# Making GpSimd wait for the VectorE copy planned before it, in an attention and gated-MLP kernel

## The chip, the cores and the metric

One core of a Trainium2 chip. The metric is the device time of one execution, in microseconds (us). A kernel was timed in several executions, and its median is quoted. On one core an execution can only be told to be slow against others of the same kernel. TensorE, VectorE (DVE in the profile), ScalarE (ACT), GpSimd (POOL) and the DMA queues are busy at the same time in the traces. The program joins them by semaphores; this case is about one more place where two of them meet.

## The reference, cut to what matters

The input has 2048 rows of 512 values. Attention with 32 heads of 16 values runs beside a gated bilinear layer of 1376 columns, and a sigmoid gate mixes the two.

```python
def reference(A_x, A_wqkv, A_wo, B_x, B_w_gate, B_w_up, B_w_down, gate_w):
    ...
        scores = jnp.einsum("bhqd,bhkd->bhqk", q, k) * (Dh ** -0.5)
        p = _softmax(scores, axis=-1)            # 32 heads x 2048 x 2048
        o = jnp.einsum("bhqk,bhkd->bhqd", p, v)
    ...
        h = g * u                                # g, u: x times w_gate, w_up
        return jnp.einsum("bsf,fd->bsd", h, w_down)
    ...
    g = _sigmoid((x * gate_w).sum(-1, keepdims=True))
    return g * a + (1 - g) * b
```

The costly part is the exponential of 134 million scores (32 x 2048 x 2048).

## The kernel before

About three quarters of the exponentials are real ones on ScalarE (line 1446). The others are made on VectorE by integer arithmetic: a score plus a constant, written as int16, has the bits of a bfloat16 power. One such operation reads PSUM (line 919, 512 columns). Three further variants of the result, with other fractional offsets, are needed; they are SBUF-to-SBUF additions on int16 (`32.0 * k`, k = 1 to 3) that the kernel calls copies. VectorE makes most of them (line 975, two tiles of 512 columns at once); GpSimd makes nearly all of those with k = 3 (line 978; 243 of 246 pairs of tiles). GpSimd also scales V (line 607) and normalises the attention output (line 1107).

No order is written by hand. The kernel file contains a planner: a small simulation with a clock for each engine, run on the host while the program is built. Whatever it decides becomes the order of each engine's queue. Which instruction waits for which comes from a list of dependencies alone. Planned times do not bind anything: on the chip, an instruction starts when its engine is free and its dependencies are met.

The planner's own rule keeps the VectorE copies and all GpSimd work apart in time, through `lock`:

```python
        def gen_step(eng):                        # one step of dve, pool, sp
            t = clock[eng]
            best = None
            if eng == "pool" and t < lock["dve"]: # a VectorE copy is running: wait
                clock[eng] = lock["dve"]
                return True
            ...                                   # best = a ready task of this queue
            if eng in ("dve", "pool") and (best is None or best.prio > 2.5):
                if eng == "pool" or lock["pool"] <= t:   # GpSimd is running: no copy
                    c = try_copy(eng, t)          # k = 1..3 on VectorE, k = 3 on GpSimd
                    if c is not None:
                        run_task(c, t)
                        lock[eng] = clock[eng]
                        return True
            ...
            qs[eng].remove(best)
            run_task(best, t)
            if eng == "pool":
                lock["pool"] = clock["pool"]
            return True
```

and in `try_copy`, the two forms of a copy (`n` is 2 but for the last one):

```python
            if eng == "dve":
                fn = lambda v: v.tensor_single_scalar(cell_ap(c, n, I16), cell_ap(pr["cell"], n, I16), 32.0 * k, ALU.add)
            else:
                fn = lambda g: g.tensor_scalar(cell_ap(c, n, I16), cell_ap(pr["cell"], n, I16), 32.0 * k, 1.0, ALU.add, ALU.mult)
            return _Task(eng, pr["p1"] + old, fn, occ, cb=cb)   # waits for its inputs and for free cells
```

The softmax here doesn't subtract the row's maximum and nothing guards it: scores larger than these inputs give would overflow.

Of the kernel before, what the change touches and what calls it, by code (L numbers as in the profile page):

```python
# [180 lines left out]
def bass_gated_mix__mha_block__glu_gated_bilinear__prompt_kernel(  # L181
    nc: bass.Bass,
    A_x: bass.AP,
    A_wqkv: bass.AP,
    A_wo: bass.AP,
    B_x: bass.AP,
    B_w_gate: bass.AP,
    B_w_up: bass.AP,
    B_w_down: bass.AP,
    gate_w: bass.AP,  # L190
    out: bass.AP,
):
    _build(nc, A_x, A_wqkv, A_wo, B_w_gate, B_w_up, B_w_down, gate_w, out)


def _build(nc, A_x, A_wqkv, A_wo, W_gate, W_up, W_down, gate_w, out):
# [29 lines left out]
    with ExitStack() as stack:  # L226
# [46 lines left out]
        def ready(task):  # L273
            r = 0.0
            for d in task.deps:
                if d.end is None:
                    return None
                e = d.end + (0.0 if d.eng == task.eng and not d.dma else SEM)
                if e > r:
                    r = e  # L280
            return r

        def run_task(task, t):
            ops = [d.op for d in task.deps]
            task.op = P.op(task.eng, task.fn, ops, task.stream, 16 if task.dma else 1)
            task.start = t
            task.end = t + task.lat
            clock[task.eng] = t + task.occ
            LOG.append(task)
            if task.cb:  # L290
                task.cb(task)
            return task
# [147 lines left out]
        PLAT = 0.44  # L440
        SW = 0.11
        pe = {"mode": "c"}
        lock = {"dve": 0.0, "pool": 0.0}

        def pe_run(deps, fn, occ, mode, t, lat=None, cb=None):
            sw = SW if mode != pe["mode"] else 0.0
# [1010 lines left out]
        def gen_step(eng):  # L1457
            t = clock[eng]
            best = None
            if eng == "pool" and t < lock["dve"]:  # L1460
                clock[eng] = lock["dve"]
                return True
            for k in qs[eng]:
                if best is not None and k.prio >= best.prio:
                    continue
                r = ready(k)
                if r is not None and r <= t:
                    if k.alloc is not None:
                        old = k.alloc(t)
                        if old is None:  # L1470
                            WHY.append((t, "p1cell"))
                            continue
                        k.deps = k.deps + old
                        k.alloc = None
                    best = k
            if eng in ("dve", "pool") and (best is None or best.prio > 2.5):
                if eng == "pool" or lock["pool"] <= t:
                    c = try_copy(eng, t)
                    if c is not None:
                        run_task(c, t)  # L1480
                        lock[eng] = clock[eng]
                        return True
            if best is None:
                return False
            qs[eng].remove(best)
            run_task(best, t)
            if eng == "pool":
                lock["pool"] = clock["pool"]
            return True
# [28 lines left out]
        for f, bk in ((f_k(0, 0, 0), slots[0][2]), (f_q(0, 0, 0), slots[1][2])):  # L1518
# [4 lines left out]
            while st["fill"] is not None:  # L1523
                do_fill(clock["pe"])

        steps = {"pe": pe_step, "act": act_step, "dve": lambda: gen_step("dve"), "pool": lambda: gen_step("pool"), "sp": lambda: gen_step("sp")}
        engs = ["pe", "act", "dve", "pool", "sp"]
        while True:
# [7 lines left out]
        def drain():  # L1536
            for _ in range(100000):
                live = [e_ for e_ in ("act", "dve", "pool", "sp") if qs[e_]]
                if not live:
                    return  # L1540
                e_ = min(live, key=lambda x: clock[x])
                if not gen_step(e_):
                    clock[e_] += 0.02
# [4 lines left out]
        c = NCH - 1  # L1548
# [19 lines left out]
        for tt in range(4):  # L1568
            cs = slice(tt * 128, (tt + 1) * 128)
            a1 = now("act", [lastpv, free], lambda a, cs=cs: a.activation(lnd[:, cs], DB.ap[:, cs], ACT.Ln), 0.2)  # L1570
            a2 = now("act", [a1], lambda a, cs=cs: a.activation(rlast[:, cs], lnd[:, cs], ACT.Exp, scale=-1.0), 0.2)  # L1571
            mt = now(
                "dve",
                [a2] + oxfree.get((NB - 1) % 2, []),
                lambda v, cs=cs: v.tensor_tensor(OX[:, (NB - 1) % 2, cs], psO[:, cs], rlast[:, cs], ALU.mult),
                0.2,
            )
            o = pe_run(
                [mt],
                col(banks[tt].ap, OX[:, (NB - 1) % 2, cs], woz[:, 1, :], False, True),  # L1580
                PACK,
                "c",
                clock["pe"],
            )
            combine(4 * c + tt, banks[tt].ap, o)
            while qs["dve"] or qs["sp"]:
                for e_ in ("dve", "sp"):
                    if qs[e_] and not gen_step(e_):
                        clock[e_] += 0.02
# [31 lines left out]
```

## Time and profile before

| | before |
|---|---|
| median of 3 runs | 803.12 us |
| profiled run, first to last instruction | 797.8 us |
| ScalarE / VectorE / TensorE / GpSimd busy | 734 / 711 / 712 / 332 us |
| mean granted TensorE clock | 0.973 |

From the page of the kernel before: the busy time of each engine; the busy tenths of VectorE and ScalarE in 40 equal slices of the execution; and three groups of instructions (line, engine, operation, output<-input, shapes, count, then busy us and mean ns, then idle time before them and what ended it).

```profile
PE 711.6 (89%) x9149; PEld 206.4 (26%) x9149; DVE 711.2 (89%) x1255; ACT 734.4 (92%) x710; POOL 331.5 (42%) x334
...
DVE  3889997789999999999999999998798999888983
ACT  3999898799999899999999999999999999889987
...
L1446 ACT ACTIVATE PT<-psS 128x1024 bf16<-128x1024 f32 (+1 forms) x572 | 614.5, 1190 | 44.5 <-PE psS L861 28.9
L978 POOL TENSOR_SCALAR PT<-PT 128x1024 int16<-128x1024 int16 x243 | 273.0, 1125 | 355.5 <-DVE PT L919 190.5
...
L975 DVE TENSOR_SCALAR PT<-PT 128x1024 int16<-128x1024 int16 (+1 forms) x498 | 276.1, 594 | 7.9 <-PE psO L1035 2.3
```

ScalarE is the busiest engine, VectorE and TensorE follow closely, and GpSimd is idle for 356 us before its copies. The 594 ns of line 975 is a mean over very unequal instructions; the view of this one line gives a minimum, median and maximum of 285, 418 and 1475 ns. Taken alone, the form with 1024 columns (groups of lines kept apart by shape, same columns):

```profile
L975 DVE TENSOR_SCALAR PT<-PT 128x1024 int16<-128x1024 int16 x495 | 275.4, 596 | 7.9 <-PE psO L1035 2.3 <-PE psS L1046 1.1
```

Why do some copies take three times as long as others of the same shape? Here is one pair, from the timelines of VectorE and of GpSimd in the same 3.5 us (start, length, engine, line; `x2` merges two in a row; the bracket has the idle time before and what ended it):

```profile
270.00 0.68 DVE L919 TENSOR_SCALAR PT<-psX 128x512 int16<-128x512 f32 x1
270.72 1.61 DVE L975 TENSOR_SCALAR PT<-PT 128x1024 int16<-128x1024 int16 x2
272.25 0.68 DVE L919 TENSOR_SCALAR PT<-psX 128x512 int16<-128x512 f32 x1
```

```profile
270.84 1.21 POOL L978 TENSOR_SCALAR PT<-PT 128x1024 int16<-128x1024 int16 x1 [1.70 <-DVE PT L919]
```

Two VectorE copies, which need 0.75 us when undisturbed (the median of 86 such pairs), take 1.61. A GpSimd copy came in 0.12 us after the first had started; the second copy is drawn out until 0.28 us after the GpSimd copy ends. A blocked VectorE instruction does not show as idle time. It shows as a longer busy one, which is why the busy share hides it.

Last, the windows view of the kernel before: busy us of each engine in each stretch of 100 us.

```profile
core 0: us, PE busy (x) PEld busy (x) DVE busy (x) ACT busy (x) POOL busy (x), PEclk, DMA share, GB/s
200.00:300.00 100.00, 90.43 (x1173) 25.15 (x1173) 97.84 (x166) 95.39 (x90) 43.89 (x38) 1.00 0.06 18
300.00:400.00 100.00, 86.23 (x1096) 24.38 (x1096) 96.92 (x169) 93.64 (x87) 44.56 (x39) 1.00 0.06 18
400.00:500.00 100.00, 95.73 (x1232) 26.09 (x1228) 93.21 (x170) 99.01 (x99) 44.20 (x39) 1.00 0.06 20
500.00:600.00 100.00, 94.56 (x1157) 25.14 (x1157) 91.43 (x167) 98.53 (x100) 43.01 (x38) 1.00 0.05 14
```

VectorE is the fullest engine from 200 to 400 us, ScalarE from 400 to 600. A kernel can have a different limit in each stretch.

Two measures, worked out from the traces instruction by instruction, are used below. *Blocked time* is, summed over the line 975 copies longer than 430 ns, what they take above 418 ns. *Lost exponential time* is, summed over the exponentials of line 1446, how much later each started after the previous one than the back-to-back pace (0.903 us at 1024 columns, 1.330 at 1536). Before, blocked time is 89 us and lost exponential time 67 us.

### The profile page before, as it was taken

How to read it: one execution, taken by the hardware profiler on the slowest of the kernel's cores; microseconds unless marked ns; L12 is line 12 of the kernel's file. 1: busy time of each engine (PE TensorE's matmuls, PEld its weight loads, DVE VectorE, ACT ScalarE, POOL GpSimd, SP SyncE). 2: the span in 40 equal slices, each digit the busy share in tenths (PEclk: the TensorE clock that was granted, in tenths of full speed). 3: DMA queues.
4: the chain of work that ended last, by engine and by line, in shares of the span. 5: the costliest groups of instructions: out<-in, count | busy, mean ns of one | idle time of the engine just before them, and what ended most of it. 6: DMA issues, size and time to landing. Idle time of an engine off the chain costs nothing. (4 is left out here: it accounts for less than half of the span.)

```text
span 797.8 us, 21597 instructions
## 1 busy us (share of the span) xinstructions
PE 711.6 (89%) x9149; PEld 206.4 (26%) x9149; DVE 711.2 (89%) x1255; ACT 734.4 (92%) x710; POOL 331.5 (42%) x334
## 2 busy tenths in 40 slices
PE   7998879988888899888799999999999988889894
PEld 3323322322222222222222222222222222222221
DVE  3889997789999999999999999998798999888983
ACT  3999898799999899999999999999999999889987
POOL 2543643144443444444435434444343444344430
PEclk9999997999999999999999999999999999899887
DMA  9700000000000010000000100000001000000000
GB/s 178 254 16 3 18 16 19 2 14 20 16 17 17 3 39 21 19 16 18 15 5 18 35 26 16 18 16 16 6 15 32 29 19 16 11 10 15 18 16 27
DMA packets 31015, 21.66 MB, mean 27 GB/s; under 512 B 18344, under 2 KB 25928, under 8 KB 30920
## 3 DMA queue, kind: packets, MB, share of 16 engines
q1 hardware_dynamic: 26936, 18.44, 7.9%
q10 hardware_dynamic: 3984, 1.84, 1.1%
q8 instruction: 73, 1.20, 0.6%
q14 instruction: 22, 0.18, 0.1%
HBM read 15.11 MB, written 2.35 MB: 22 GB/s over the span
## 5 line engine op out<-in xcount | busy, mean ns | idle before, releaser
L1446 ACT ACTIVATE PT<-psS 128x1024 bf16<-128x1024 f32 (+1 forms) x572 | 614.5, 1190 | 44.5 <-PE psS L861 28.9
L978 POOL TENSOR_SCALAR PT<-PT 128x1024 int16<-128x1024 int16 x243 | 273.0, 1125 | 355.5 <-DVE PT L919 190.5
L861 PE MATMUL psS<-QM,KE 32*128 32x512 bf16 x1732 | 273.4, 391 | 17.1 <-ACT PT L1446 9.5
L975 DVE TENSOR_SCALAR PT<-PT 128x1024 int16<-128x1024 int16 (+1 forms) x498 | 276.1, 594 | 7.9 <-PE psO L1035 2.3
L1035 PE MATMUL psO<-PT,VS 128*18 128x512 bf16 x1791 | 241.0, 390 | 6.1 <-DVE PT L975 2.7
L919 DVE TENSOR_SCALAR PT<-psX 128x512 int16<-128x512 f32 x316 | 214.6, 679 | 28.1 <-PE psS L861 24.8
L1035 PE MATMUL psO<-PT,VD 128*18 128x512 bf16 x1479 | 227.6, 387 | 9.2 <-DVE PT L975 4.8
L861 PE MATMUL psX<-QM,KE 32*128 32x512 bf16 x316 | 122.5, 388 | 24.6 <-DVE PT L919 10.9
L1446 ACT ACTIVATE wv<-psS 128x1024 bf16<-128x1024 f32 (+1 forms) x117 | 134.1, 1160 | 6.7 <-PE psS L861 6.2
L919 DVE TENSOR_SCALAR PT<-psS 128x512 int16<-128x512 f32 x177 | 118.8, 679 | 11.2 <-PE psS L861 9.0
L861 PEld LDWEIGHTS psS<-QM,KE 32*128 32x128 bf16 x1732 | 67.4, 91 | 167.6 <-ACT PT L1446 68.4
L1035 PE MATMUL psO<-wv,VS 128*18 128x512 bf16 x257 | 71.9, 393 | 1.3 <-POOL PT L978 1.0
L1035 PEld LDWEIGHTS psO<-PT,VS 128*18 128x18 bf16 x1791 | 56.7, 89 | 62.8 <-issue 31.8
L861 PEld LDWEIGHTS psX<-QM,KE 32*128 32x128 bf16 x316 | 28.7, 91 | 152.2 <-DVE PT L919 71.9
L1035 PEld LDWEIGHTS psO<-PT,VD 128*18 128x18 bf16 x1479 | 52.6, 88 | 56.9 <-issue 32.7
L492 PE MATMUL psS<-xT,wu 128*32 128x512 bf16 x672 | 55.1, 391 | 2.2 <-DVE hT L707 1.3
L492 PE MATMUL psS<-xT,wg 128*32 128x512 bf16 x672 | 52.6, 384 | 3.8 <-DVE PT L919 1.4
L492 PE MATMUL psS<-wd,hT 128*32 128x512 bf16 (+1 forms) x704 | 53.0, 386 | 2.3 <-DVE PT L919 2.3
L1107 POOL TENSOR_TENSOR OT<-oraw,rb 128x512 bf16<-128x512 f32 x16 | 20.6, 1284 | 38.2 <-DMA rb<-rscr 38.1
L675 DVE CAST usb<-psS 128x512 bf16<-128x512 f32 (+1 forms) x43 | 29.1, 677 | 1.8 <-PE psS L492 1.8
L707 DVE TENSOR_TENSOR hT<-psS,usb 128x512 bf16<-128x512 f32 (+1 forms) x43 | 29.1, 677 | 1.7 <-PE psS L492 1.6
L1107 POOL TENSOR_TENSOR OX<-oraw,rb 128x512 bf16<-128x512 f32 x15 | 19.1, 1272 | 23.1 <-DMA rb<-rscr 23.1
(87 smaller groups left out, 339.1 us busy)
## 6 DMA issues: line engine op xcount, KB each, us to landing
rb<-rscr SPq DMA_DIRECT2D x31, 256.0 KB
out_dram<-ost SPq DMA_DIRECT2D x16, 128.0 KB, 1.7
wu<-in_B_w_up_dram SPq DMA_DIRECT2D x1, 1376.0 KB, 7.5
wg<-in_B_w_gate_dram SPq DMA_DIRECT2D x1, 1376.0 KB, 10.6
wd<-in_B_w_down_dram SPq DMA_DIRECT2D x1, 1280.0 KB, 12.4
OT<-OX SPq DMA_DIRECT2D x60, 16.0 KB, 1.8
wv<-in_A_wqkv_dram ACTq DMA_DIRECT2D x2, 256.0 KB, 7.8
wo<-in_A_wo_dram SPq DMA_DIRECT2D x1, 512.0 KB, 8.6
```

The costliest lines, as they stand in the source:

```text
L492: return e.matmul(out_ap[32 * q : 32 * q + w, :], lhs[:, 32 * q : 32 * q + w], rhs, start=s0, stop=s1, tile_position=(0, 32 * q), skip_gro ...
L675: lambda v: v.tensor_copy(usb[0:w, n % 2, :], bk.ap[0:w, :]),
L707: lambda v: v.tensor_tensor(hT[0:w, f, :], bk.ap[0:w, :], usb[0:w, n % 2, :], ALU.mult),
L861: r = e.matmul(bk.ap, KE[32 * j : 32 * j + 32, b, kt * 128 : (kt + 1) * 128], QM[32 * j : 32 * j + 32, p, b, :], start=True, stop=True, ti ...
L919: lambda v: v.tensor_scalar(cell_ap(pr["cell"] + i, 1, mybir.dt.int16), bk.ap, CB, 0.0, ALU.add, ALU.max),
L975: fn = lambda v: v.tensor_single_scalar(cell_ap(c, n, I16), cell_ap(pr["cell"], n, I16), 32.0 * k, ALU.add)
L978: fn = lambda g: g.tensor_scalar(cell_ap(c, n, I16), cell_ap(pr["cell"], n, I16), 32.0 * k, 1.0, ALU.add, ALU.mult)
L1035: r = e.matmul(psO[32 * j : 32 * j + VW, :], pv_stationary(m, kt, j, k), cell_ap(cell, 1), start=s0, stop=s1, tile_position=(0, 32 * j), s ...
L1107: lambda e: e.tensor_tensor(dst, oraw[:, s, :], rb[:, s, :], ALU.mult),
L1446: lambda a: a.activation(cell_ap(c, n), src, ACT.Exp, scale=LN2 / 128.0),
```

## The change

The intent: the planner keeps GpSimd and the VectorE copies apart, but the chip does not know it. So each GpSimd operation is given one dependency more, on the VectorE copy planned last before it.

```diff
-        lock = {"dve": 0.0, "pool": 0.0}
+        lock = {"dve": 0.0, "pool": 0.0, "op": None}
...
                     c = try_copy(eng, t)
                     if c is not None:
+                        if eng == "dve":
+                            lock["op"] = c
+                        elif lock["op"] is not None:
+                            c.deps.append(lock["op"])
                         run_task(c, t)
...
             qs[eng].remove(best)
+            if eng == "pool" and lock["op"] is not None:
+                best.deps.append(lock["op"])
             run_task(best, t)
```

The planner's decisions do not depend on it. The work and the order of every queue stay as they were. Only GpSimd's waits change.

## The prediction

> **What bounds the kernel now.** The page gives ScalarE 734 us busy (92% of 797.8), VectorE 711 (89%), TensorE 712 (89%), GpSimd 332 (42%). In the trace, back-to-back exponentials (line 1446) start 0.903 us apart at 1024 columns and 1.330 us at 1536; the 689 of them would take 698 us at that pace, but stretch over 764: 67 us are lost. The windows view shows where. From 200 to 400 us VectorE is the limit: 98 and 97 us busy per 100, ScalarE 95 and 94, 17 us of exponential time lost. From 400 to 600 ScalarE is 99% busy and loses 7 us.
>
> **Why VectorE is so full.** Its 495 SBUF-to-SBUF copies of 1024 columns (line 975) last 418 ns in the median but 596 in the mean. Setting them against the GpSimd spans: 168 copies start while a GpSimd operation is already running; they average 948 ns and end some 0.28 us after it. 113 overlap but started first; they average 419 ns. The Trainium skill (SBUF — State Buffer, section "SBUF: two separate sides") says that GpSimd and a VectorE operation in a two-port mode take an exclusive lock and the loser fully blocks. This trace agrees: the copies pay 89 us above 418 ns. Matched to the planned order, 158 of 241 GpSimd copies start before the copy planned ahead of them has ended, typically by 1.5 us: the plan keeps the two apart but doesn't enforce it. Pairs in the wrong order cost 67 us of the 89; the other 22 are copies that overtake a GpSimd operation planned before them.
>
> **What the change does.** No instruction and no order changes; GpSimd's waits rise to a later VectorE count. GpSimd operations of the wrong order start 1 to 1.5 us later; with 356 us idle before its copies it can afford that. It removes about 67 us of blocked copies and gives some back: GpSimd now starts right behind a copy and holds the lock about 1.05 us; two PSUM reads of VectorE (0.598 us apart) cover that, one doesn't. From the order and these durations I estimate 10 us of that, on top of the 22. So VectorE falls from 711 to about 655 us busy, and 25 to 45 us of blocking remain.
>
> **How much is on the critical path.** Only where VectorE limits. If 200 to 400 us loses as little as 400 to 600, that is 10 us; 600 to 750, where 20 us are blocked and 15 of exponential time lost, perhaps 8; 100 to 200, where TensorE's projections and a lower clock matter too, perhaps 4; the rest 1. Sum about 23 us.
>
> **Predicted: 780 us, range 768 to 793.** Chances: faster by over 2% 0.78, within 2% 0.20, slower by over 2% 0.02.
>
> **What would show it.** Right: line 975 copies near 480 ns in the mean; blocked excess under 45 us; VectorE about 655 us busy, ScalarE 94 to 95%; GpSimd copies waiting for line 975; TensorE's waits for GpSimd results under 20 us. Wrong: the copies' mean stays above 550 (collisions only moved to the next copy); or the mean falls but 200 to 400 us loses the same exponential time (something else limits); or TensorE waits for GpSimd tiles.
>
> **What would make it wrong.** Delayed GpSimd operations may hit the next copy instead; later tiles may hold TensorE or tile cells longer; a denser TensorE may be granted a lower clock (0.973 now, 0.90 to 0.93 in two stretches).

## The result, and the profile after

| | before | after |
|---|---|---|
| median of 4 runs | 802.41 us | 771.93 us |
| profiled run | 797.8 us | 767.6 us |
| mean granted TensorE clock | 0.973 | 0.977 |
| blocked time of the line 975 copies | 89 us | 30 us |
| lost exponential time | 67 us | 37 us |

The ratio of after to before is 0.962, with a 95% interval of 0.959 to 0.965: faster. Ratios here and below divide the mean time of one kernel's fast runs by that of the other's in the same rounds, so they are not quite the ratio of the medians. Executions over 1.5% slower than the fastest of the same kernel are left out of the means.

The same lines of the page after:

```profile
PE 707.3 (92%) x9149; PEld 207.6 (27%) x9149; DVE 658.8 (86%) x1255; ACT 727.6 (95%) x710; POOL 314.4 (41%) x334
...
DVE  3889896689898999999989989898788989989882
ACT  3999988898999999999999999999999999999987
...
L1446 ACT ACTIVATE PT<-psS 128x1024 bf16<-128x1024 f32 (+1 forms) x572 | 614.2, 1240 | 25.9 <-PE psS L861 13.0
L978 POOL TENSOR_SCALAR PT<-PT 128x1024 int16<-128x1024 int16 x243 | 256.1, 1055 | 359.7 <-DVE PT L975 226.4
...
L975 DVE TENSOR_SCALAR PT<-PT 128x1024 int16<-128x1024 int16 (+1 forms) x498 | 217.2, 476 | 6.6 <-PE psO L1035 1.2
```

The instruction counts are the same. VectorE does the same work in 52 us less busy time: line 975 fell by 59, and a few us came back in other lines. GpSimd's idle time before its copies hardly grew (355.5 to 359.7 us), but what ends it has changed: the VectorE copy, line 975. GpSimd's copies became shorter too (1125 to 1055 ns), since a GpSimd copy that arrives during a VectorE copy is blocked in its turn: before, the 136 that started during one averaged 1190 ns, the other 107 averaged 1043; after, only 8 started during one. ScalarE waits 26 us in place of 45 at line 1446.

The same pair of copies after, with the GpSimd copy of the same place in the plan:

```profile
263.29 1.14 DVE L975 TENSOR_SCALAR PT<-PT 128x1024 int16<-128x1024 int16 x2
264.74 0.69 DVE L919 TENSOR_SCALAR PT<-psX 128x512 int16<-128x512 f32 x1 [0.30 <-PE psS L861]
```

```profile
262.78 1.04 POOL L978 TENSOR_SCALAR PT<-PT 128x1024 int16<-128x1024 int16 x1 [1.76 <-DVE PT L975]
264.52 1.04 POOL L978 TENSOR_SCALAR PT<-PT 128x1024 int16<-128x1024 int16 x1 [0.69 <-DVE PT L975]
```

The GpSimd copy starts at 264.52, behind both VectorE copies, which end at 264.43, and beside operations that read PSUM. What blocking remains is also to be seen: the first of the two VectorE copies met the GpSimd copy before this one, which ran until 263.82, and the pair took 1.14 us in place of 0.75.

And the windows:

```profile
200.00:300.00 100.00, 95.19 (x1248) 26.73 (x1240) 91.66 (x175) 99.03 (x96) 43.66 (x40) 1.00 0.07 22
300.00:400.00 100.00, 92.95 (x1198) 26.55 (x1190) 93.21 (x183) 99.79 (x94) 44.45 (x42) 1.00 0.05 15
400.00:500.00 100.00, 97.43 (x1224) 26.13 (x1221) 91.89 (x176) 99.93 (x103) 41.94 (x39) 1.00 0.07 23
500.00:600.00 100.00, 95.62 (x1187) 25.78 (x1184) 85.71 (x163) 99.05 (x100) 40.83 (x38) 1.00 0.06 17
```

From 200 to 400 us ScalarE is now 99% busy, as it already was from 400 to 600. VectorE has handed the limit to ScalarE there.

Set against the planned times (the planner was run on the host, and its list paired with the trace in the order of each queue), the execution before fell further and further behind: 2.5 us behind at the start, 21 us at 400 us, 37 us near the end of the main part. After, it stays 4 to 6 us behind from 200 to 720 us. That is a picture of what happened, not yet a proof of its cause.

### The profile page after: what moved, and what is told of

Same layout as the page of the kernel before. It is cut to its first block, busy times and chain, and to the rows that moved or that the text cites. A ratio compares the mean times of both kernels' runs of the same rounds, so it can differ in the third digit from the quotient of the medians.

```text
span 767.6 us, 21608 instructions
## 1 busy us (share of the span) xinstructions
PE 707.3 (92%) x9149; PEld 207.6 (27%) x9149; DVE 658.8 (86%) x1255; ACT 727.6 (95%) x710; POOL 314.4 (41%) x334
## 5 line engine op out<-in xcount | busy, mean ns | idle before, releaser
L978 POOL TENSOR_SCALAR PT<-PT 128x1024 int16<-128x1024 int16 x243 | 256.1, 1055 | 359.7 <-DVE PT L975 226.4
L975 DVE TENSOR_SCALAR PT<-PT 128x1024 int16<-128x1024 int16 (+1 forms) x498 | 217.2, 476 | 6.6 <-PE psO L1035 1.2
L1446 ACT ACTIVATE wv<-psS 128x1024 bf16<-128x1024 f32 (+1 forms) x117 | 138.2, 1201 | 2.1 <-PE psS L861 2.0
```

Source lines behind the costliest of these rows:

```text
L1446: lambda a: a.activation(cell_ap(c, n), src, ACT.Exp, scale=LN2 / 128.0),
```

## The experiments

Two theories were put against each other. The *lock theory*: GpSimd and a VectorE copy exclude each other; GpSimd in the wrong order blocks copies; and a blocked copy costs time only where VectorE limits. Its rivals: that holding GpSimd back helps in some other way (pacing), that enforcing the plan from either side would do, and that every microsecond of blocking costs the same. All runs had 5 rounds. In each set of four they shared one chip and the runs of the kernel before. The medians of before in the three sets were 803, 800 and 803 us.

| run | ratio to before (95% interval) | blocked time |
|---|---|---|
| the change (first measurement) | 0.962 (0.959 to 0.965) | 30 us |
| e1_copies_only | 0.968 (0.963 to 0.973) | 32 us |
| e2_others_only | 1.002 (0.997 to 1.008) | 89 us |
| e3_dve_waits | 1.045 (1.040 to 1.050) | 79 us |
| e4_both_wait | 0.994 (0.989 to 0.999) | 0 us |
| e5_short_before (wrong result) | 0.956 (0.952 to 0.960) | 17 us |
| e6_short_after (wrong result) | 0.956 (0.953 to 0.960) | 11 us |
| e7_middle | 0.984 (0.980 to 0.988) | 70 us |
| e8_later | 0.997 (0.992 to 1.002) | 73 us |
| f0_after_again | 0.965 (0.962 to 0.969) | 28 us |
| f1_tail | 0.959 (0.956 to 0.963) | 31 us |
| f2_tail_fill | 0.947 (0.943 to 0.951) | 28 us |
| f3_wait_copies | 0.979 (0.975 to 0.983) | 5 us |

### Which GpSimd operations carry the gain: e1 and e2

The edits to the changed kernel, each taking away one of the two new waits (first e1, then e2):

```diff
-            if eng == "pool" and lock["op"] is not None:
-                best.deps.append(lock["op"])
```

```diff
-                        elif lock["op"] is not None:
-                            c.deps.append(lock["op"])
```

> Only the GpSimd copies (line 978) wait for the latest VectorE copy; the normalising multiplies and the V scalings do not. Lock theory (GpSimd in the wrong order blocks VectorE copies): before, 93 of the 99 wrong-order blockings and 66 of their 67 us came from GpSimd copies, so nearly the whole gain stays: ratio to before 0.960 to 0.967, blocked excess 28 to 34 us. Rival (any holding back of GpSimd, or the changed waits of the multiplies, is what helps): clearly less gain, 0.97 or more.

> Only the other GpSimd operations (multiplies, V scalings) wait for the latest VectorE copy; the GpSimd copies do not. Lock theory: under 1 us of wrong-order blocking came from them, so almost nothing: ratio 0.996 to 1.003, blocked excess 85 to 90 us, mean of the line 975 copies 585 to 600 ns. Rival: if the multiplies' timing carried the gain, 0.98 or less.

The wait of the GpSimd copies alone gives a ratio of 0.968, just outside the expected 0.960 to 0.967, with an interval that overlaps that of the full change (0.965 when it was run again). With the three slow runs of the kernel before left in, it would be 0.966, so this miss says little. The wait of the others alone gives nothing: 1.002, and the copies' mean stays at 595 ns. The gain is that of the GpSimd copies.

### Whether it is the length of the hold: e5 and e6

In the kernel before and in the changed one, GpSimd's copies were cut to 128 of 1024 columns. Their outputs are wrong, which doesn't matter for the times. The plan and the waits stay, and the target cells are cleared once at the start so that nothing unwritten is read.

```diff
-  g.tensor_scalar(cell_ap(c, n, I16), cell_ap(pr["cell"], n, I16), 32.0 * k, 1.0, ALU.add, ALU.mult)
+  g.tensor_scalar(cell_ap(c, n, I16)[:, 0:128], cell_ap(pr["cell"], n, I16)[:, 0:128], 32.0 * k, 1.0, ALU.add, ALU.mult)
```

> Wrong result on purpose: the kernel before, with the GpSimd copies doing 128 columns of 1024 (about 0.3 us in place of 1.04; the same plan, the same waits, the target cells cleared once at the start). No new wait. Lock theory (the time that GpSimd holds the lock is what costs): blocked excess falls from 89 to under 25 us and the time to 0.955 to 0.972 of before. Rival (the wait paces GpSimd or TensorE's order in some other way): no wait is added, so 0.99 to 1.0.

> Wrong result on purpose: the changed kernel with the same short GpSimd copies as e5. Lock theory: with short holds the wait has nothing left to save: within 0.6% of e5_short_before, 0.955 to 0.970 of before. Rival (the wait helps by pacing): 2 to 4% faster than e5_short_before.

Both came out at 0.956, medians 765.2 and 765.4 us. With short holds and no new wait, the kernel before is as fast as the changed one; with short holds the wait adds nothing. Pacing as the cause is ruled out: e5 has none, and e6 has it and gains nothing from it. How long GpSimd holds a copy up is what cost the time. One thing more differs in e5: short copies also hand their results on sooner. That can't be the main part: TensorE's waits for GpSimd results were about 15 us in all before the change and about 15 after it, and the change gained 30 us without shortening them. The changed kernel lies at 0.962 to 0.965 on two chips, within about 1% of this pair; that hints at how little the remaining blocking costs, but it is no bound, since e6 still has 11 us of blocking and the pair ran on another chip.

### Where a blocked microsecond costs time: e7 and e8

The change for the GpSimd operations planned from 190 to 380 us (e7) or from 380 to 600 us (e8) alone; both new waits got the condition, shown for e7:

```diff
-                        elif lock["op"] is not None:
+                        elif lock["op"] is not None and 190.0 <= t < 380.0:
```

> The change only for GpSimd operations planned between 190 and 380 us (about 200 to 400 us of the execution before). Critical-path theory (blocking costs time only where VectorE limits): this stretch lost 23 us of blocking to the change and gives 11 to 15 us, ratio 0.981 to 0.987. Rival (every us of blocking costs alike, 30 us of time for 60 of blocking): also about 11 us; the pair with e8_later tells them apart by time gained per us of blocking removed.

> The change only for GpSimd operations planned between 380 and 600 us (about 400 to 625 us before), where ScalarE was 99% busy. Critical-path theory: about 11 us of blocking go, but only 1 to 4 us of time: ratio 0.995 to 0.999, under 0.35 us of time per us of blocking. Rival (every us of blocking costs alike, 0.5): 5 to 6 us, ratio 0.992 to 0.994.

In e7, 19 us of blocking went and the ratio is 0.984: 1.6% of 800 us, 13 us. In e8, 17 us of blocking went (the expectation had said 11) and the ratio is 0.997: about 2 us, and its interval contains 1. By these totals that is 0.68 us of time for each blocked us where VectorE was the limit and 0.13 where ScalarE was. But the totals also hold what differed by chance outside the stretch. Counted by planned time inside it, e7 took away 21.0 us of blocking and 11.6 us of lost exponential time, 0.55 us per us; e8 took away 12.7 and 3.4, 0.27 per us. The full change gives 0.56 and 0.31 in the same two stretches. So a blocked us cost about twice as much where VectorE was the limit, and it was not free where ScalarE was. The rival of equal worth had expected 0.992 to 0.994 for e8; the interval just touches it at 0.992. With the 12.7 us that went in the stretch, equal worth at 0.5 would have been 6 us, again 0.992: e8's time alone makes equal worth unlikely but does not exclude it, and the counts by stretch speak against it.

### Enforcing the order from the other side: e3, e4 and f3

In e3, VectorE copies wait for the latest GpSimd operation planned before them, and GpSimd waits for nothing new. In e4, both sides wait. In e4 the edit to the changed kernel is:

```diff
                         if eng == "dve":
                             lock["op"] = c
-                        elif lock["op"] is not None:
-                            c.deps.append(lock["op"])
+                            if lock["gop"] is not None:
+                                c.deps.append(lock["gop"])
+                        else:
+                            lock["gop"] = c
+                            if lock["op"] is not None:
+                                c.deps.append(lock["op"])
...
                 lock["pool"] = clock["pool"]
+                lock["gop"] = best
```

> The reverse: each VectorE copy waits for the latest GpSimd operation planned before it; GpSimd waits for nothing new. Lock theory: this only turns the 22 us of blockings in the planned order into waits of the same length, and leaves the 67 us of wrong-order blockings: ratio 0.995 to 1.012, blocked excess 62 to 75 us, VectorE idle up by some 20 us. Rival (enforcing the planned order from either side is what helps): 0.97 to 0.985.

> The change as it is, and each VectorE copy also waits for the latest GpSimd operation planned before it. Lock theory: blocked excess falls from 30 us to under 5, but a semaphore wait takes its place, so no gain over the change: ratio to before 0.960 to 0.970. Rival (the 30 us of blocking that the change leaves still cost time and can be had by full order): 0.95 or less.

Both expectations missed, and in a direction that neither theory had. e3 is 4.5% slower than before. e4 has no blocking left at all (mean of the copies 421 ns) and has lost nearly the whole gain. The profile says where it went. The groups by shape and the waits of VectorE in e4 (who waited <- for whom: us in total, times, longest):

```profile
L975 DVE TENSOR_SCALAR PT<-PT 128x1024 int16<-128x1024 int16 x495 | 187.6, 421 | 68.6 <-POOL PT L978 32.8 <-POOL OT L1107 11.9 <-POOL VD L607 6.7
```

```profile
DVE PT L975 <- POOL PT L978: 32.8, 40, 2.9
...
DVE PT L975 <- POOL OT L1107: 11.9, 8, 2.8
...
DVE PT L975 <- POOL VD L607: 6.7, 5, 2.9
DVE PT L975 <- POOL OX L1107: 5.5, 4, 2.8
```

The 30 us of blocking that the change had left became 57 us of idle waiting (32.8 + 11.9 + 6.7 + 5.5). The trace of e4 shows two causes. First, the hand-over is later: a copy released by the semaphore starts 105 ns (median of 90) after GpSimd's recorded end. A blocked copy ends 0.28 us after GpSimd's end and takes 0.418 alone, so it gets going 0.14 us *before* that end. The semaphore therefore costs about 0.245 us more each time, by these numbers; 71 copies of e4 waited for a GpSimd operation that already ran. Second, a semaphore also waits for an operation that has not begun: 19 copies did, for about 33 us in all. The lock lets such a copy pass.

In e3 the same two things come on top of the blockings in the wrong order, which stay: VectorE's idle time rises by 43 us (84 to 127) and blocked time falls by only 11. The net 32 us are close to the 35 us by which the profiled execution became longer.

To test this explanation, f3 takes out of e4 the waits for all GpSimd operations but the copies:

```diff
                 lock["pool"] = clock["pool"]
-                lock["gop"] = best
```

> Follows up e4, which lost the gain: there VectorE idled 57 us for GpSimd in place of 30 us of blocking, 24 of it for multiplies and V scalings, which themselves wait for DMAs. Here VectorE copies wait for the latest GpSimd copy alone. If idling behind a semaphore in place of the lock is what e4 lost by (copies start 105 ns after GpSimd's end, not 140 ns before it, and wait for operations that have not begun): about 33 us of idling against 21 of blocking, 8 to 14 us slower than the changed kernel, 0.972 to 0.982 of before. If the loss came from the multiplies alone: within 3 us of the changed kernel.

It came out at 0.979, and 11 us slower than the changed kernel on the same chip (785.8 to 774.8), as the explanation had it. VectorE idled 41 us for GpSimd copies (33 expected) where 23 us of blocking went (28 to 5). So the waits for the multiplies and V scalings are one part of e4's loss and the semaphore in place of the lock another. The two causes within that second part were read from the trace, not separated by a run.

### A faster version: f1 and f2

After the change ScalarE is 98% busy or more in each 100 us from 200 to 700, so what is left there is on ScalarE. At the end of the program four Ln activations alternate with four Exp, and each change loads a table. The changed kernel, timeline of ScalarE near the end:

```profile
760.48 1.28 ACT L1576 ACT_TABLE_LOAD   x1
761.78 0.28 ACT L1576 ACTIVATE oraw<-psS 128x128 f32<-128x128 f32 x1
762.07 1.28 ACT L1577 ACT_TABLE_LOAD   x1
763.37 0.31 ACT L1577 ACTIVATE rb<-oraw 128x128 f32<-128x128 f32 x1
```

f1 puts the four Ln ahead of the four Exp. f2 also changes one threshold of the planner.

```diff
+        a1s = []
         for tt in range(4):
             cs = slice(tt * 128, (tt + 1) * 128)
-            a1 = now("act", [lastpv, free], lambda a, cs=cs: a.activation(lnd[:, cs], DB.ap[:, cs], ACT.Ln), 0.2)
+            a1s.append(now("act", [lastpv, free], lambda a, cs=cs: a.activation(lnd[:, cs], DB.ap[:, cs], ACT.Ln), 0.2))
+        for tt in range(4):
+            cs = slice(tt * 128, (tt + 1) * 128)
+            a1 = a1s[tt]
             a2 = now("act", [a1], lambda a, cs=cs: a.activation(rlast[:, cs], lnd[:, cs], ACT.Exp, scale=-1.0), 0.2)
...
-        FA0 = 12
+        FA0 = 20                                 # f2 only
```

> The changed kernel once more, as the yardstick of this chip: 0.958 to 0.968 of before.

> The changed kernel with the last block's four Ln activations ahead of its four Exp activations. In the trace after the change, 8 table loads of 1.28 us alternate with them on the chain that ends last; 2 remain, so 6 x 1.28 = 7.7 us less one wait for the three other Ln (about 0.9 us): 6 to 8 us faster than the changed kernel, 0.949 to 0.959 of before. If the tail's ScalarE chain were not what ends last, under 2 us.

> f1 with one planner threshold changed (20 in place of 12 for putting projections into the third score bank), which the kernel's own plan makes 7.6 us shorter. Lock theory: with GpSimd held to the plan the execution follows the plan (4 to 6 us behind it from 200 to 720 us), so the plan's gain arrives: 4 to 9 us faster than f1. Rival (the plan says little about the chip): within 3 us of f1.

f1's median is 4.7 us below that of the changed kernel (774.8 to 770.2); 6 to 8 were expected, and the ratio of 0.9594 is just above the expected 0.959. ScalarE in f1:

```profile
754.84 1.28 ACT L1581 ACT_TABLE_LOAD   x1
756.13 0.91 ACT L1581 ACTIVATE rb<-oraw 128x128 f32<-128x128 f32 x4
```

The loads did go; the last exponential of the softmax to the end of the program takes 14.6 us in place of 19.0. But from ScalarE's last activation to the end it is 8.1 us in place of 4.0. The four output blocks used to be finished one by one while ScalarE loaded tables; now all four are released at once and queue behind VectorE and TensorE. f2 came to 759.0 us, 0.947 of before, 11 us below f1 where 4 to 9 were expected. In the profiled runs f2 ends about 6 us behind its plan and f1 10, so of the 12 us between these two runs 7.6 are the plan's: that gain did arrive. The other 4 are a smaller lag that no run explains. It is the fastest version here. Two limits of this: the threshold was picked by the plan's own length, and f2 was not run without the new wait, so that the wait is what makes the plan trustworthy is argued, not shown, for this last step.

## Why the prediction was right

- **The limit, right.** From 200 to 400 us VectorE was to be the limit. After the change ScalarE went there from 95 and 94 us to 99 and 100 of each 100, and e7 shows that this stretch pays.
- **The cause, right, and tested.** That GpSimd in the wrong order blocks the copies: e1, e2 and e5, e6 decide against the rivals put forward. The page "SBUF — State Buffer" of the Trainium skill, section "SBUF: two separate sides", says that the loser of the shared port pair fully blocks; here a copy that met a running GpSimd operation averaged 948 ns, one that came first 419. The page "VectorE: DVE Perf Modes", section "Why PSUM operands drop a tier", says that a mode using both SBUF ports is closed to operands in PSUM. This agrees with line 919, which reads PSUM and stays between 673 and 691 ns (10th to 90th percentile); the 252 of its 493 instructions that GpSimd ran beside lie between 673 and 692, the others between 672 and 691.
- **The residual, right.** 10 us given back on top of 22 were estimated, 32 in all; 30 remained: 18 on copies that had been blocked in the planned order before, 12 on others. So two small misses partly cancel. VectorE was put at about 655 us busy (659 measured), the copies at 480 ns in the mean (477), ScalarE at 94 to 95% (95), TensorE's waits for GpSimd results under 20 us (15).
- **The share on the critical path, too small.** 23 us were predicted and 30 came, within the range given (768 to 793). The mis-sized term is the stretch-by-stretch sum. Cutting the exponentials into the same blocks in both traces, with the blocks' times of before: to 183 us lost time fell by 4.4 us (about 5 predicted); from 183 to 407 by 12.1 (10); from 407 to 605 by 3.3 (nearly 0); from 605 on by 11.0 (8). The stretch limited by ScalarE was not quite free of VectorE's delays, and the exponentials of 200 to 400 us lost even less afterwards (4.3 us) than the stretch taken as their yardstick (7 us from 400 to 600). e7 and e8 agree for the middle ones (13 and 2 us); what the last stretch gives was not tested by itself.
- **The feared clock, unfounded here.** TensorE was 92% busy in place of 89%, and its mean clock was 0.977 in place of 0.973.

## What to carry to other kernels

When the same instruction has very unequal lengths in a trace, set the long ones against what the other engines ran at that moment: blocked time counts as busy and no list of waits shows it. A planned order binds nothing that no dependency enforces; where two engines exclude each other, holding back the one that has idle time is cheap, and making the scarce one wait as well can cost more than the lock itself, because a semaphore hands over later and also waits for work that has not begun. What a removed stall is worth depends on which engine limits its stretch: here, counted inside the stretch, 0.55 us per us in one (e7) and 0.27 in another (e8).

## What the Trainium skill lacked or had wrong

- "SBUF — State Buffer", section "SBUF: two separate sides": it gives the exclusive lock and a hand-over time for GpSimd's DMA descriptors after a VectorE operation, but none for a VectorE operation after a GpSimd one. Here a blocked copy ended 0.28 us after GpSimd's recorded end, with 0.418 us of its own: it gets going about 0.14 us before that end. The page has the pair held for the whole instruction; by the recorded spans, which the profile calls rough for GpSimd, it is free a little earlier.
- No page that was read says that the lock can be cheaper than a semaphore in the same place. Here it was: 105 ns after GpSimd's end in place of 140 before it, and 11 us (f3) and some 20 us (e4, against e1 on the same chip) lost by adding the semaphore.
- "Perfetto Trace Analysis", section "Optimizing Scalar/DVE Operations", warns that moving work between VectorE and GpSimd might not help because of the shared port. Here the same split of work became 3.8% faster by ordering alone. The section lacks how a blocked operation looks: busy, at 948 ns in place of 418.
- "ScalarE: Activation LUTs", section "What ACT_TABLE_LOAD costs", puts a change of tables at 2.66 us with a drain. Here the load was 1.28 us, as it says, but the next activation started 0.02 us after it, so a change cost about 1.3 us. Its section "Table sets: the hidden batching unit" has Ln and then Exp in one set with one load; this program loaded a table at every change between the two, 8 times.
